# Spectral mixing and a squared-ReLU FFN on one Trainium2 core: the seven-product form for sixteen more token groups, complex sums and casts moved to DMAs

## The chip, the cores and the metric

The kernel runs on one core of one Trainium2 chip. The metric is the device time of one execution in microseconds (us); lower is better. The kernel before took 789.52 us (median of three runs, 789.43 to 789.87). The granted clock of TensorE was 1.000 in the profiled execution.

A core has five engines with a queue each, worked off in order: PE (TensorE, the matrix engine; PEld is its weight load), DVE (VectorE), ACT (ScalarE), POOL (GpSimd) and SP (SyncE, which issues most transfers here). They wait for one another through semaphores.

## The reference

```python
# x (8, 3008, 256), filt_r and filt_i (1505, 256), moe_w_in (256, 2048), moe_w_out (2048, 256), all float32
X = np.fft.rfft(x, axis=1)
Y = X * (filt_r + 1j * filt_i)[None, :, :]
y = np.fft.irfft(Y, n=3008, axis=1).astype(np.float32)
h = np.maximum(y.reshape(24064, 256) @ moe_w_in, 0.0)
out = (h * h @ moe_w_out).astype(np.float32)
```

Each of the eight batch elements is filtered along its 3008 positions; then all 24064 tokens go through a two-layer network whose activation is the squared ReLU.

## The kernel before, in words

**The FFN.** The tokens are worked off in 47 groups of 512. A group has eight *slots*, s = 8g + k. In slot k, `ffn_g1` (line 562) makes four matmuls of 512 columns, which give two of the sixteen 128-row tiles of the hidden layer; ACT applies the ReLU from PSUM into `h2` (line 566); `ffn_sq` squares the two tiles in place on DVE (line 570). The second layer runs one group late: in the slots of group g+1, `ffn_g2` (line 579) makes eight matmuls of 256 columns for group g in each slot, with a tile of `h2` as the weights and `sWout` as the moving operand; `ffn_out` copies the sum out of PSUM twice a group (line 590), and `store` issues its transfers (lines 610 and 612).

**The seven-product form.** For the groups in `SEVEN` (40 to 45 before), the second layer is written as a 2 x 2 by 2 x 2 block product: two halves of the tokens, two halves of the hidden rows, two halves of the output columns. `sums` makes four sums of blocks of `h2` on DVE (lines 643 to 652), and `make_t` makes the four sums of blocks of `sWout` once. `products` then forms seven products of sixteen matmuls of 128 columns each, instead of 64 of 256 columns (line 670). `PARTS` spreads them over eight slots, one slot later than `ffn_g2` would: slots 1 to 7 of group g+1 and slot 0 of group g+2. Two PSUM tiles, `psX` and `psY`, are held from the first product to the last. ACT copies four of the seven results out (lines 677 to 689), and DVE makes three additions (lines 686, 687, 692).

**The mixing.** It is a DFT in two factors (64 x 47), and every batch element passes five stages. x is loaded as float32 by SP (line 192) and cast to float16 by DVE (line 340). *Stage A* (`unit_a`, line 361) is the 47-point part; its output goes through DRAM (`write_u` line 344, `read_u` line 436) for a transposition. *Stage B* (`unit_b`, line 445) is the other factor for two of the 24 frequency classes at a time; DVE multiplies it by the filter (line 453), which gives `prod`, of which the partner's half stands in the other 64 partitions. Two DVE copies bring it across (lines 460 and 461), and `unit_s` adds (line 467): that is the sum of a complex product. *Stage P* (`unit_p`, line 496) goes back, ACT copies it out (line 498), and it passes through DRAM (`dZ`, line 501; `read_z`, line 514). *Stage Y* (`unit_y`, line 532) finishes and writes the tokens `yt` that `ffn_g1` reads.

**What sets the order.** The order is written out by hand: the last loop of the kernel goes through the slots, and in each it issues `ffn_g1`, the mixing work planned for place 0, the second layer of the group before, the mixing work of place 1, then `ffn_out`, `sums` and `ffn_sq`. `fft_plan(b)` gives each unit of batch element b a slot r counted from a start; the starts of b = 2 to 7 lie 48 slots, six groups, apart (b = 3 starts at slot 88). There stage A has the slots r = 6 to 13, `read_u` 14, stage B 19 to 37, `unit_p` two slots after its `unit_b`, `read_z` 40, stage Y 45 to 52. Batch element 0 is worked off before the loop, in a prologue; b = 1 is interleaved with the first groups. Stages A, B, P and Y share two PSUM banks (`psF`); `psH` has two buffers of two banks, `psO` two of one bank.

Of the kernel before, what the change touches and what calls it, by code (L numbers as in the profile page):

```python
# [110 lines left out]
def kernel(  # L111
# [32 lines left out]
    p_prod = ctx.enter_context(tc.tile_pool(name="p_prod", bufs=3))  # L144
    p_yf = ctx.enter_context(tc.tile_pool(name="p_yf", bufs=4))
# [3 lines left out]
    p_out = ctx.enter_context(tc.tile_pool(name="p_out", bufs=3))  # L149

# [33 lines left out]
    x32s = {}  # L184

    def load_x(b, c, pool=None, tag="x32", q=None):

        t = (pool or p_x32).tile([96, 8, D], F32, tag=tag, name=f"x32_{b}_{c}")
        q = q or nc.sync
        if b + 1 < B:  # L190
            v = xrows[b * S:b * S + 96 * NM, :].rearrange("(p m) d -> p m d", m=NM)
            q.dma_start(out=t, in_=v[:, 8 * c:8 * c + 8, :])
        else:
            v = xrows[b * S:b * S + S, :].rearrange("(p m) d -> p m d", m=NM)
            q.dma_start(out=t[0:80], in_=v[0:80, 8 * c:8 * c + 8, :])
            q.dma_start(out=t[80:94], in_=v[80:94, 8 * c:8 * c + 8, :])
        x32s[(b, c)] = t
# [3 lines left out]
    sC0 = const.tile([128, 1472], F16, name="sC0")  # L201
# [3 lines left out]
    sSA = sC0[0:94, 1280:1376]  # L205
    sSY = sC0[0:112, 1376:1470]
# [40 lines left out]
    nc.sync.dma_start(out=sC0[:, 704:1472], in_=dC0.ap()[:, 704:1472])  # L247
# [60 lines left out]
    def load_win():  # L308

        for k, c, n, pool, tag in ((0, 0, 768, p_ze, "ze"), (0, 768, 768, p_ze, "ze"),  # L310
                                   (0, 1536, 512, p_prod, "prod"), (1, 0, 768, p_ze, "ze"),
                                   (1, 768, 512, p_prod, "prod"), (1, 1280, 512, p_prod, "prod"),
                                   (1, 1792, 256, p_yf, "yf")):
            t = pool.tile([128, n], F32, tag=tag, name=f"win32_{k}_{c}")
            nc.sync.dma_start(out=t, in_=moe_w_in[128 * k:128 * k + 128, c:c + n])
            wins.append((t, k, slice(c, c + n)))
# [19 lines left out]
    x16s, us, uts, prods, zes, zts, yts = {}, {}, {}, {}, {}, {}, {}  # L336

    def cast_x(b, c, eng=nc.vector):
        t = p_x16.tile([94, 8, D], F16, tag="x16", name=f"x16_{b}_{c}")
        eng.tensor_copy(out=t, in_=x32s.pop((b, c))[0:94])  # L340
        x16s[(b, c)] = t

# [5 lines left out]
    def unit_a(b, a):  # L348

        c, i = divmod(a, 4)  # L350
        if i == 0:
            us[(b, c)] = p_u.tile([96, 8, D], F16, tag="u", name=f"u_{b}_{c}")
        ps = psF(f"psA_{b}_{a}")
        m = slice(2 * i, 2 * i + 2)
        if b == 1:
            nc.tensor.matmul(ps[0:96, :], s1[:, c // 2, :], xw16[(b, 2 * (c % 2))][:, m, :],
                             start=True, stop=False)
            nc.tensor.matmul(ps[0:96, :], s1[0:120, 2 + c, :], xw16[(b, 1)][0:120, m, :],
                             start=False, stop=True)
        else:  # L360
            nc.tensor.matmul(ps[0:96, :], sSA, x16s[(b, c)][:, m, :], start=True, stop=True)  # L361
        o = us[(b, c)][:, 2 * i:2 * i + 2, :]
        pv = ps[0:96, :].rearrange("p (a d) -> p a d", d=D)
        if a % 2 == 0:
            nc.scalar.copy(out=o, in_=pv)  # L365
        else:
            nc.vector.tensor_copy(out=o, in_=pv)  # L367
        if i == 3:
            write_u(b, c)
# [69 lines left out]
    def unit_b(b, p):  # L439
# [18 lines left out]
        if b > 0:  # L458
            yf = p_yf.tile([128, 2, D], F16, tag="yf", name=f"yf_{b}_{p}")
            nc.vector.tensor_copy(out=yf[0:64], in_=prod[64:128, 1])  # L460
            nc.vector.tensor_copy(out=yf[64:128], in_=prod[0:64, 1])
            prods[(b, p)] = prod, yf

    def unit_s(b, p):

        prod, yf = prods[(b, p)]
        nc.vector.tensor_add(out=yf, in0=prod[:, 0], in1=yf)  # L467
        prods[(b, p)] = yf
# [20 lines left out]
    def unit_p(b, p):  # L489
# [3 lines left out]
        yf = prods.pop((b, p))  # L493
# [12 lines left out]
    ztiles = [const.tile([112, 8, D], F16, name=f"zt_{c}") for c in range(4)]  # L506
# [3 lines left out]
    def read_z(b, c, ks=(0, 1)):  # L510
        zt = ztiles[c]
        v = dZ[b].rearrange("(q j) d -> q j d", j=NM)
        for k in ks:
            nc.sync.dma_start(out=zt[64 * k:64 * k + 48],
                              in_=v[48 * k:48 * k + 48, 8 * c:8 * c + 8, :])
        zts[(b, c)] = zt
# [51 lines left out]
    def ffn_sq(g, s):  # L568
        v = h2s[g][:, 2 * s:2 * s + 2, :]
        nc.vector.tensor_mul(out=v, in0=v, in1=v)  # L570
# [46 lines left out]
    def make_t():  # L617

        t = p_x32.tile([128, 4, 8, 128], F16, tag="x32", name="sT")
# [13 lines left out]
    def sums(g, k):  # L633
# [7 lines left out]
        t = p_x16.tile([128, 8, D], F16, tag="x16", name=f"sum_{g}_{k}")  # L641
# [17 lines left out]
    def products(g, k):  # L659

        f = sg[g]
        for p, m0, m1 in PARTS[k]:
# [12 lines left out]
            if p == 1:  # L675
                f["pu"] = p_prod.tile([128, 2, 2, 128], F32, tag="prod", name=f"pu_{g}")
                nc.scalar.copy(out=f["pu"][:, 0], in_=o)
            elif p == 6:
                f["u2"] = p_prod.tile([128, 2, 128], F32, tag="prod", name=f"u2_{g}")
                nc.scalar.copy(out=f["u2"], in_=o)  # L680
            elif p == 7:
                nc.scalar.copy(out=f["pu"][:, 1], in_=o)
            elif p == 2:
                f["top"] = p_out.tile([128, 2, 256], F32, tag="ost", name=f"top_{g}")
                f["bot"] = p_out.tile([128, 2, 256], F32, tag="ost", name=f"bot_{g}")
                nc.vector.tensor_add(out=f["top"][:, :, 0:128], in0=f["y"][:, 0], in1=f["pu"][:, 0])
                nc.vector.tensor_add(out=f["bot"][:, :, 128:256], in0=f["y"][:, 1], in1=f["pu"][:, 1])
            elif p == 4:
                nc.scalar.copy(out=f["bot"][:, :, 0:128], in_=o)
                store(g, 2, 2, f["bot"])  # L690
            elif p == 3:
                nc.vector.tensor_add(out=f["top"][:, :, 128:256], in0=o, in1=f["u2"])
                store(g, 0, 2, f["top"])

    def fft_plan(b):
# [11 lines left out]
        t0 = 2 if b == 1 else 6  # L707
        for a in range(12 if b == 1 else 0, 16):
            put(t0 + a // 2, a % 2, unit_a, b, a)
        put(10 if b == 1 else 14, 1, read_u, b)  # L710
        t0 = 14 if b == 1 else 19
        for p in range(12):
            r = t0 + (17 if b == 1 else 18) * p // 11
            put(r, 0, unit_b, b, p)
            put(r, 0, unit_s, b, p)
            put(r + 2, 1, unit_p, b, p)
        t0 = 34 if b == 1 else 40
        for c in range(4):
            put(t0, 1, read_z, b, c)
        if b + 1 < B:  # L720
            for c in range(2):
                put(t0 - 13, 1, load_x, b + 1, c)
            for c in range(4):
                r = t0 - 8 + 3 * c
                put(r, 1, cast_x, b + 1, c)
                if c < 2:
                    put(r, 1, load_x, b + 1, c + 2)
# [79 lines left out]
    SEVEN = range(40, NG - 1)  # L807
    work = {}
    for b in range(1, B):
        first = (b * S // TG) * SLOTS - (48 if b > 1 else 40)  # L810
        for (r, place), w in fft_plan(b).items():
            work[(first + r, place)] = w
# [49 lines left out]
```

## Time and profile before

| what | value |
|---|---|
| median of the runs (lowest, highest) | 789.52 us (789.43, 789.87) |
| the profiled execution's own time | 789.29 us |
| its span from first to last instruction | 787.2 us |
| around the span | 2.1 us |
| DMA traffic | 107.36 MB, mean 136 GB/s |
| SP's queue, share of 16 DMA engines | 46.9% |
| POOL busy, nearly all of it in the first 50 us | 23.6 us |
| loop over the slots, from its first matmul | 49.2 us on |

How to read it: the profile has the busy time of each engine, then groups of instructions by source line (busy time, mean duration of one in ns, the engine's idle time before them and what ended it), then the chain of work that ended last. A matmul's duration in it covers its whole way through the array, so that of a row of matmuls each starts long before the one ahead has ended. What a matmul costs TensorE is the distance from start to start, which the timeline shows. Beside POOL's own instructions, the issue of a DMA by POOL appears as an instruction, `DMA_DIRECT2D`.

### The profile page before, as it was taken

The numbers are of one execution on the slowest core, as the hardware profiler recorded it, in microseconds if no ns is written. First come the engines' busy times: TensorE is split into PE (matmuls) and PEld (weight loads), VectorE is DVE, ScalarE is ACT, GpSimd is POOL, SyncE is SP. The second block draws the span as 40 slices with busy tenths as digits, with TensorE's granted clock in tenths as the row PEclk, the third lists the DMA queues.
The fourth block names the chain that finished last, engine by engine and source line by source line (L and its number), as shares of the span: only waits on it lengthen the run. The fifth ranks groups of instructions, "written<-read, shape, count | busy, mean of one in ns | idle before, by whom it ended". The sixth has DMA issues, their size and how long they took to land.

```text
span 787.2 us, 15477 instructions
## 1 busy us (share of the span) xinstructions
PE 774.9 (98%) x6390; PEld 552.6 (70%) x6390; DVE 584.4 (74%) x943; ACT 558.5 (71%) x723; POOL 23.6 (3%) x36
## 2 busy tenths in 40 slices
PE   8989999999999999999999999999999999999998
PEld 5846667667676676867778677776767667677776
DVE  6866995579855897559965599556995569878884
ACT  3976776777777776767776777676777767777674
POOL 3800000000000000000000000000000000000000
PEclk9999999999999999999999999999999999999999
DMA  9995554345724467054571555525564342421011
GB/s 363 371 258 157 147 158 112 88 139 158 193 67 109 158 169 181 32 160 145 134 186 49 169 141 140 148 67 161 147 169 98 91 138 82 109 67 54 29 54 55
DMA packets 88574, 107.36 MB, mean 136 GB/s; under 512 B 6336, under 2 KB 79040, under 8 KB 84288
## 3 DMA queue, kind: packets, MB, share of 16 engines
q1 hardware_dynamic: 88296, 106.19, 46.9%
q8 instruction: 50, 0.82, 0.4%
q10 hardware_dynamic: 144, 0.18, 0.1%
q14 instruction: 20, 0.16, 0.1%
q0 software_dynamic: 64, 0.00, 0.0%
HBM read 58.12 MB, written 48.23 MB: 135 GB/s over the span
## 4 chain that ended last, share of the span: by engine, by line
PE 91%; DVE 6%; ACT 1%; DMA 1%; issue 0%; ACTq 0%; SPq 0%; DVEq 0%
PE psH L562 39%; PE psO L579 34%; PE psX L670 3%; PE psA L361 3%; PE psY L532 2%; PE psB L445 2%; PE psP L496 2%; PE psY L670 2%; DVE prod L453 2%; DVE h L570 2%; PE warm L268 1%; DMA wout<-in_moe_w_out_dram 1%; PE psf L287 1%; PE psf L290 1%; DVE yf L467 0%; ACT sF L298 0%
## 5 line engine op out<-in xcount | busy, mean ns | idle before, releaser
L566 ACT ACTIVATE h<-psH 128x1024 f16<-128x1024 f32 x376 | 384.9, 1025 | 183.1 <-PE psH L562 180.5
L562 PE MATMUL psH<-yt,sWin 128*128 128x512 f16 (+7 forms) x1728 | 386.9, 351 | 1.7 <-DVE yt L541 0.7
L579 PE MATMUL psO<-sWout,h 128*128 128x256 f16 x2624 | 339.2, 272 | 0.6 <-DVE h L570 0.6
L570 DVE TENSOR_TENSOR h<-h 128x1024 f16<-128x1024 f16 x376 | 251.9, 684 | 66.3 <-ACT h L566 65.6
L579 PEld LDWEIGHTS <-h 128*128 128x128 f16 x2624 | 253.3, 98 | 66.0 <-DVE h L570 0.9
L562 PEld LDWEIGHTS <-sWin 128*128 128x128 f16 x1728 | 157.7, 98 | 100.7 <-issue 3.4
L453 DVE TENSOR_TENSOR prod<-psB,sF 128x1024 f16<-128x1024 f32 x84 | 102.3, 1218 | 2.8 <-PE psB L445 2.7
L541 DVE CAST yt<-psY 128x376 f16<-128x376 f32 x62 | 34.0, 549 | 54.7 <-PE psY L532 54.6
L367 DVE CAST u<-psA 96x512 f16<-96x512 f32 x50 | 34.3, 687 | 47.3 <-PE psA L361 45.1
L498 ACT CAST ze<-psP 128x512 f16<-128x512 f32 x84 | 49.1, 585 | 17.2 <-PE psP L496 14.7
L590 ACT COPY ost<-psO 128x512 f32<-128x512 f32 (+1 forms) x84 | 48.8, 581 | 7.7 <-PE psO L579 4.3
L532 PE MATMUL psY<-sC,zt 112*128 112x94 f16 x512 | 42.3, 205 | 1.0 <-DMA zt<-dZ 1.0
L532 PEld LDWEIGHTS <-zt 112*128 112x128 f16 x512 | 34.9, 98 | 11.1 <-issue 1.2
L467 DVE TENSOR_TENSOR yf<-prod,yf 128x512 f16<-128x512 f16 x84 | 35.7, 425 | 2.9
L361 PE MATMUL psA<-x,sC 94*96 94x512 f16 x96 | 36.6, 382 | 0.0
L445 PE MATMUL psB<-ut,sSB 128*128 128x256 f16 x192 | 36.5, 273 | 0.0
L496 PE MATMUL psP<-yf,sSP 128*128 128x256 f16 x168 | 32.1, 272 | 0.5 <-DVE prod L453 0.3
L445 PEld LDWEIGHTS <-sSB 128*128 128x128 f16 x192 | 18.5, 98 | 19.5
L539 ACT CAST yt<-psY 128x376 f16<-128x376 f32 x66 | 30.9, 468 | 1.6 <-issue 1.3
L340 DVE CAST x<-x 94x2048 f16<-94x2048 f32 x24 | 29.2, 1216 | 0.0
L365 ACT CAST u<-psA 96x512 f16<-96x512 f32 x50 | 28.6, 572 | 0.0
L670 PEld LDWEIGHTS <-sum 128*128 128x128 f16 x384 | 23.8, 98 | 4.9
(88 smaller groups left out, 395.3 us busy)
## 6 DMA issues: line engine op xcount, KB each, us to landing
x<-in_x_dram SPq DMA_DIRECT2D x20, 768.0 KB
zt<-dZ SPq DMA_DIRECT2D x64, 192.0 KB
dU<-u SPq DMA_DIRECT2D x28, 384.0 KB
dZ<-ze SPq DMA_DIRECT2D x28, 384.0 KB
out_dram<-ost SPq DMA_DIRECT2D x58, 128.0 KB
ut<-dU SPq DMA_DIRECT2D x7, 1024.0 KB
out_dram<-ost SPq DMA_DIRECT2D x27, 256.0 KB
xw<-in_x_dram SPq DMA_DIRECT2D x6, 1024.0 KB
```

What stands on the lines that cost most here:

```text
L361: nc.tensor.matmul(ps[0:96, :], sSA, x16s[(b, c)][:, m, :], start=True, stop=True)
L445: nc.tensor.matmul(ps[:, i * D:(i + 1) * D], sSB[:, 2 * p + i, :], uts[b][:, 2 * p + i, :], start=True, stop=True)
L453: nc.vector.tensor_mul(out=prod, in0=ps.rearrange("p (a d) -> p a d", d=D).unsqueeze(1).to_broadcast([128, 2, 2, D]), in1=sF[:, :, 2 * p:2 ...
L496: nc.tensor.matmul(ps[:, i * D:(i + 1) * D], sSP[:, 2 * p + i, :], yf[:, i, :], start=True, stop=True)
L498: nc.scalar.copy(out=zes[(b, c)][:, 2 * i6:2 * i6 + 2, :], in_=ps.rearrange("p (a d) -> p a d", d=D))
L532: nc.tensor.matmul(ps[:, 94 * jj:94 * jj + 94], zt[:, 4 * (g % 2) + jj, dt * 128:(dt + 1) * 128], sSY, start=True, stop=True)
L562: nc.tensor.matmul(ps[:, i, o:o + n], sWin[:, dt, jt * 128:(jt + 1) * 128], yts[b][:, dt, r:r + n], start=(dt == 0), stop=(dt == 1))
L566: nc.scalar.activation(out=h2[:, 2 * s:2 * s + 2, :], in_=ps, func=AF.Relu)
L570: nc.vector.tensor_mul(out=v, in0=v, in1=v)
L579: nc.tensor.matmul(pso[g][:, t % 2, :], h2s[g][:, jt, t * 128:(t + 1) * 128], sWout[:, jt, :], start=(jt == 0), stop=(jt == NJT - 1))
L590: nc.scalar.copy(out=ost[:, h0:h0 + step, :], in_=pso[g][:, h0:h0 + step, :])
L670: nc.tensor.matmul(o[:, t, :], f[p][:, q, 128 * t:128 * t + 128], sg["w"][p][:, q, :], start=(m == 0 and p in (1, 2)), stop=(q == 7), skip ...
```

## The change

- **Seven products for more groups.** `SEVEN` gains the odd groups 9 to 39, sixteen in all. A plain group follows each of them, so that slot 0 of the group after a seven-product group has `ffn_g1` alone, and slot 0 of the next has the last part of `products` and the first of `ffn_g2`.
- **Squares over two slots.** `ffn_sq` does four tiles in every second slot, but for the last group.
- **Adding DMAs.** The two copies and the addition on DVE after the filter product go. POOL issues two DMAs of 64 x 512 elements each that add one half of `prod` onto the other in place. `unit_p` comes four slots after its `unit_b` instead of two, and `prod` has four buffers instead of three.
- **x cast by its DMAs.** SP's loads of x and DVE's casts go. POOL issues eight DMAs for each batch element (for the last one sixteen) that read float32 and write float16, one after each of eight of the `unit_b` of the batch element before.
- **Moves.** Stages A and B and `read_u` come one slot earlier, `read_z` one slot later (41), and the read of its last quarter at slot 47, because three tiles `zt` serve instead of four. For b = 1, stage B is spread over 15 slots instead of 17.
- **Memory.** The first and the seventh result, and the sixth, are copied by ACT straight into the tiles `top` and `bot` that are stored, and DVE adds there. The sums lie in the pool that held the loads of x. One constant is loaded in two parts.

The core of the diff:

```diff
@@ def load_x
-    def load_x(b, c, pool=None, tag="x32", q=None):
-        t = (pool or p_x32).tile([96, 8, D], F32, tag=tag, name=f"x32_{b}_{c}")
-        q = q or nc.sync
+    def load_x(b, k):
+        c, i = divmod(k, 2)
+        if i == 0:
+            x16s[(b, c)] = p_x16.tile([96, 8, D], F16, tag="x16", name=f"x16_{b}_{c}")
+        t = x16s[(b, c)][:, 4 * i:4 * i + 4, :]
+        m = slice(8 * c + 4 * i, 8 * c + 4 * i + 4)
         if b + 1 < B:
             v = xrows[b * S:b * S + 96 * NM, :].rearrange("(p m) d -> p m d", m=NM)
-            q.dma_start(out=t, in_=v[:, 8 * c:8 * c + 8, :])
+            nc.gpsimd.dma_start(out=t, in_=v[:, m, :])
...
-    def cast_x(b, c, eng=nc.vector):
-        t = p_x16.tile([94, 8, D], F16, tag="x16", name=f"x16_{b}_{c}")
-        eng.tensor_copy(out=t, in_=x32s.pop((b, c))[0:94])
-        x16s[(b, c)] = t
@@ def unit_b
         if b > 0:
-            yf = p_yf.tile([128, 2, D], F16, tag="yf", name=f"yf_{b}_{p}")
-            nc.vector.tensor_copy(out=yf[0:64], in_=prod[64:128, 1])
-            nc.vector.tensor_copy(out=yf[64:128], in_=prod[0:64, 1])
-            prods[(b, p)] = prod, yf
-
-    def unit_s(b, p):
-        prod, yf = prods[(b, p)]
-        nc.vector.tensor_add(out=yf, in0=prod[:, 0], in1=yf)
-        prods[(b, p)] = yf
+            for i in range(2):
+                nc.gpsimd.dma_start(out=prod[64 * i:64 * i + 64, 0],
+                                    in_=prod[64 - 64 * i:128 - 64 * i, 1],
+                                    accum_op=mybir.AluOpType.add)
@@ def ffn_sq
-        v = h2s[g][:, 2 * s:2 * s + 2, :]
+        n = 1 if g == NG - 1 else 2
+        if (s + 1) % n:
+            return
+        v = h2s[g][:, 2 * (s + 1 - n):2 * s + 2, :]
         nc.vector.tensor_mul(out=v, in0=v, in1=v)
@@ def products
             if p == 1:
-                f["pu"] = p_prod.tile([128, 2, 2, 128], F32, tag="prod", name=f"pu_{g}")
-                nc.scalar.copy(out=f["pu"][:, 0], in_=o)
+                f["top"] = p_out.tile([128, 2, 256], F32, tag="ost", name=f"top_{g}")
+                nc.scalar.copy(out=f["top"][:, :, 0:128], in_=o)
...
             elif p == 2:
-                f["top"] = p_out.tile([128, 2, 256], F32, tag="ost", name=f"top_{g}")
-                f["bot"] = p_out.tile([128, 2, 256], F32, tag="ost", name=f"bot_{g}")
-                nc.vector.tensor_add(out=f["top"][:, :, 0:128], in0=f["y"][:, 0], in1=f["pu"][:, 0])
-                nc.vector.tensor_add(out=f["bot"][:, :, 128:256], in0=f["y"][:, 1], in1=f["pu"][:, 1])
+                for v, i in ((f["top"][:, :, 0:128], 0), (f["bot"][:, :, 128:256], 1)):
+                    nc.vector.tensor_add(out=v, in0=f["y"][:, i], in1=v)
@@ def fft_plan
-        t0 = 2 if b == 1 else 6
+        t0 = 2 if b == 1 else 5
...
-        put(10 if b == 1 else 14, 1, read_u, b)
-        t0 = 14 if b == 1 else 19
+        put(10 if b == 1 else 13, 1, read_u, b)
+        t0 = 14 if b == 1 else 18
         for p in range(12):
-            r = t0 + (17 if b == 1 else 18) * p // 11
+            r = t0 + (15 if b == 1 else 18) * p // 11
             put(r, 0, unit_b, b, p)
-            put(r, 0, unit_s, b, p)
-            put(r + 2, 1, unit_p, b, p)
-        t0 = 34 if b == 1 else 40
+            if b + 1 < B and 2 <= p < 10:
+                put(r, 0, load_x, b + 1, p - 2)
+            put(r + 4, 1, unit_p, b, p)
+        t0 = 34 if b == 1 else 41
         for c in range(4):
-            put(t0, 1, read_z, b, c)
...
+            put(t0 if c < 3 else t0 + 6, 1, read_z, b, c)
@@ the loop
-    SEVEN = range(40, NG - 1)
+    SEVEN = [g for g in range(9, NG - 1) if g % 2 or g >= 40]
```

## Prediction

> **What bounds the kernel now.** I read the busy times first, then the groups, then TensorE's timeline in a stretch without mixing work.
>
> ```profile
> PE 774.9 (98%) x6390; PEld 552.6 (70%) x6390; DVE 584.4 (74%) x943; ACT 558.5 (71%) x723; POOL 23.6 (3%) x36
> L579 PE MATMUL psO<-sWout,h 128*128 128x256 f16 x2624 | 339.2, 272 | 0.6 <-DVE h L570 0.6
> L570 DVE TENSOR_TENSOR h<-h 128x1024 f16<-128x1024 f16 x376 | 251.9, 684 | 66.3 <-ACT h L566 65.6
> L453 DVE TENSOR_TENSOR prod<-psB,sF 128x1024 f16<-128x1024 f32 x84 | 102.3, 1218 | 2.8 <-PE psB L445 2.7
> L467 DVE TENSOR_TENSOR yf<-prod,yf 128x512 f16<-128x512 f16 x84 | 35.7, 425 | 2.9
> L340 DVE CAST x<-x 94x2048 f16<-94x2048 f32 x24 | 29.2, 1216 | 0.0
> ```
>
> TensorE is never idle for long, so time comes off only where its own work does. In the timeline (start, length, instructions) the next two fences show a plain slot and slots of groups 42 to 45, which are in the seven-product form already:
>
> ```profile
> 206.00 1.03 PE L562 MATMUL psH<-yt,sWin 128*128 128x512 f16 x4
> 206.86 1.04 PE L579 MATMUL psO<-sWout,h 128*128 128x256 f16 x8
> 207.73 1.03 PE L562 MATMUL psH<-yt,sWin 128*128 128x512 f16 x4
> ```
>
> ```profile
> 742.79 1.03 PE L562 MATMUL psH<-yt,sWin 128*128 128x512 f16 x4
> 743.66 0.61 PE L670 MATMUL psX<-sT,sum 128*128 128x128 f16 x8
> 744.10 0.50 PE L670 MATMUL psY<-sT,sum 128*128 128x128 f16 x6
> 744.44 0.38 PE L562 MATMUL psH<-yt,sWin 128*128 128x512 f16 x1
> ```
>
> A plain slot is 1.74 us from start to start, one with 14 small products 1.65. The third view is busy time by stretch, for one group under seven products without mixing and for two groups in stage B (columns: stretch, its length, then PE, PEld, DVE, ACT):
>
> ```profile
> 736.21:749.37 13.16, 13.16 (x147) 9.39 (x145) 10.81 (x15) 9.33 (x13) 0.00 (x0) 1.00 0.13 42
> 269.22:285.08 15.86, 15.86 (x117) 11.16 (x114) 15.45 (x29) 11.87 (x16) 0.00 (x0) 1.00 0.67 183
> 285.08:300.94 15.86, 15.86 (x117) 11.12 (x115) 15.35 (x26) 11.62 (x15) 0.00 (x0) 1.00 0.52 135
> ```
>
> DVE is 97% busy in stage B. Four sums more would not fit there; that is why the change must first empty DVE.
>
> **What the Trainium skill says.** "TensorE: Matmul & The Clock Gate", section "Wait — 56ns, not 53.3ns?": a warm matmul starts N/2.4 ns + 2.5 ns after the one ahead. The trace agrees: 216, 109 and 56 ns from start to start at 512, 256 and 128 columns, weight loads hidden. "DMA: Bandwidth & Descriptors", section "Anatomy of one DMA": a DMA from GpSimd takes 2.0 us plus its bytes over 436 GB/s; 2.15 us for 64 KB. Its section "Latency and other measured facts" puts about 1 us on the issue. The trace has only two tiny ones, at its busy start: 617 and 484 ns to issue, 6.2 us to land. "SBUF — State Buffer", section "Who interferes with whom": a two-input DVE operation does not keep GpSimd from writing descriptors, a copy or cast within SBUF can. The change removes those copies; no row of before shows the two together.
>
> **The change, part by part.**
>
> *Seven products.* A plain group takes 8 x 1.738 = 13.90 us, a seven-product group 13.16 (window above): 0.74 less; by the gaps, 64 x 0.109 - 112 x 0.056 = 0.70. Sixteen groups: **-11.9**. The short slot (`ffn_g1` alone, 0.87) and the long one (0.87 + 12 x 0.056 + 0.87 = 2.4) move work, and add none. ACT needs 1.02 for a ReLU in the short slot, but the two `psH` buffers carry 0.15 over: nothing.
>
> *DVE.* Off: casts 29.2, copies 24.3 + 24.1, additions 35.7, together 113 us; squares in pairs cost a step of 1.135 (as the sums have) against 2 x 0.602: -3. On: 64 sums x 1.218 = 78, 48 additions x 0.42 = 20. DVE falls from 584 to about 555, but it waits beside TensorE, so this is worth only what DVE holds up now. That is in b = 1, where the timeline has
>
> ```profile
> 93.36 0.38 PE L496 MATMUL psP<-yf,sSP 128*128 128x256 f16 x2 [0.27 <-DVE prod L453]
> 113.67 0.39 PE L579 MATMUL psO<-sWout,h 128*128 128x256 f16 x2 [0.60 <-DVE h L570]
> ```
>
> From start to start these cost 0.44 and 0.76; with DVE's backlog gone: **-1.2**.
>
> *DVE where seven products meet stage B.* For b = 3 to 7 one group (13, 19, ... 37) has its products in r = 25 to 32, with five `unit_b`. I add up both queues from r = 24 on (DVE steps 1.135 for squares, sums, products with the filter; PE 0.87 `ffn_g1`, 0.22 each B and P, parts at 0.056 a matmul). Slots start at 0, 1.1, 3.1, 5.1, 7.0, 8.9, 11.0, 12.7, 14.7. DVE: square 0.4, prod 1.5, sum 2.65, sum 3.9, square 5.0, prod 6.2, sum 7.3, prod 8.5 to 9.7, square, sum, prod 11.9, square, two additions 14.2, prod 14.9 to 16.1. It runs up to 2 us late, yet each sum is ready (the first at 3.9 for 4.8, the second at 5.1 for 6.5). What is late is the PSUM bank: the `unit_b` of r = 29 needs the prod done at 9.7 and comes at 9.8; that of r = 32 comes at 15.6 and needs 16.1. **+0.5** x 5 = 2.5 (0 to 1.2 each). The other ten groups meet stage A or Y, where DVE has 0.6 or 0.47 us a slot instead: nothing, covered by 0.3 us at least.
>
> *Adding DMAs.* Off TensorE's path while they land before `unit_p`: four slots, about 7.2 us after the prod; 5.1 and 4.8 in r = 30 and 31 above, where prod is late. Price: from 2 x 0.5 + 2.15 = 3.2 to 2 x 1.0 + 6.2 = 8.2. An early landing gains nothing, since `unit_p` has its place in PE's queue. I take 2 x 0.9 and 2.6 for the landing, as SP's write of `dZ` has it: 4.4, with 0.3 lost in some of the tight places: **+1.5** (0 to 4). What queues behind: the next adding DMA waits for its prod, and the loads of x stand between; unit_p's wait holds PE's whole queue. DVE waits before it reuses a `prod` buffer for the DMAs of four units earlier, whose `unit_p` is through by then: nothing.
>
> *x cast by DMAs.* 24 loads leave SP's queue, whose waits cost nothing now. On POOL each comes behind two adding DMAs, so three issues in each 3.3 us (1.64 slots of 2.0). At 0.9 us they fit. Needed 20 slots later: nothing.
>
> *Stage P to Y.* Here a cover shrinks. Before (b = 3), the last `unit_p` ends at 301.1; `dZ` is written, and the first two reads of `zt` follow:
>
> ```profile
> 301.75 0.38 SPq L501 DMA_DIRECT2D dZ<-ze  x1
> 302.24 1.71 SPq L612 DMA_DIRECT2D out_dram<-ost  x3
> 304.05 3.81 SPq L514 DMA_DIRECT2D zt<-dZ  x8
> 310.48 0.33 PE L532 MATMUL psY<-sC,zt 112*128 112x94 f16 x4
> ```
>
> By the trace's semaphore updates `dZ` landed at 304.75 and the second read at 308.23, 2.25 us early (1.1 to 2.3 over b = 2 to 7). After, `unit_p` stands in r = 40, a short slot, and r = 41 to 44 are slots with products (1.76, 1.65, 1.65, 1.65): from its end to `unit_y` it is 7.4 us instead of 9.4. ACT has the ReLU of that slot ahead of its copy: 1.3 until `dZ` is issued, then 0.4 + 2.6 + 0.35 + 2.95 (medians) = 7.6. **+0.3** with the scatter, for six batch elements: 1.8 (0 to 1.2 each). The read at slot 47 has four slots of some 2 us for 3.3: nothing.
>
> *Rest.* One more small load in the prologue, results copied straight into `top`: same counts, nothing.
>
> Sum: 789.3 - 11.9 - 1.2 + 2.5 + 1.5 + 1.8 = 782.0 in the profiled execution's own time; the median of the runs stands 0.2 higher, **782.2**.
>
> **The rivals.**
>
> *No stall* (0.16): queues fit as written, 789.5 - 13.1 = 776.4. For it: groups 41 to 45 run without a wait. Against: in none of them is there mixing.
>
> *The waits take it* (0.16): both ends above, 6 + 4 + 7.2 = 17.2 instead of 5.8, some of which fall together; with 11.5, 787.9. For it: a DVE 2 us late and a cover of 7.4 us for 7.6.
>
> *Slower: POOL's issue is the bound* (0.16). From b = 1 to 6 there are eight spells of three issues in 3.29 us. Above 1.10 us an issue, POOL falls behind by 8 x (3x - 3.29), of which `unit_p` has 7.2 - 4.6 = 2.6 to give; the rest TensorE waits. It decides from 1.26 us: 8 x 0.49 - 2.6 = 1.3 us, six times, which is the 7.3 gained. At 1.4 us: 8 x 0.91 - 2.6 = 4.7, six times 28, 810. For it: 1 us by the skill, for one DMA of unknown shape. Against: 0.5 to 0.6 in the trace.
>
> **How the numbers follow.** My forecast has 0.52. About 0.2% (1.6 us) is what a measurement of this kernel can tell from no change. The second rival lies half within that (0.07), nearly all else of it below (0.08). Faster 0.52 + 0.16 + 0.08 = 0.76, same 0.07, slower 0.17. The range goes from the stall-free end, 776, to the upper end of the waits, 790; outside are the slower rival and little else.
>
> **What would show it.** Slots of 1.65 us with parts of products in groups 10 to 40, and 1.74 elsewhere: the saving. Idle time of PE at `unit_b` put down to the filter product: the bank. At `unit_y`, to `zt`: the shrunk cover. At `unit_p`, to a DMA into `prod`, with POOL's `DMA_DIRECT2D` over 1.1 us: the slower rival. I am wrong if a DVE operation or a matmul changes its own duration beside POOL's DMAs, or if landings of the adding DMAs take over 5 us.

## The result, and the profile after

| | before | after |
|---|---|---|
| median of the runs (lowest to highest) | 789.56 us (789.43 to 789.87) | 789.68 us (787.49 to 791.16) |
| ratio, 95% interval | | 0.9999 (0.9975 to 1.0023) |
| the profiled execution's own time; its span | 789.29; 787.2 us | 791.16; 789.1 us |

No change that can be measured, where 782.2 was forecast. The page of the changed kernel first, the busy times and the groups that answer to those shown of before:

```profile
PE 766.1 (97%) x7158; PEld 552.1 (70%) x7158; DVE 548.0 (69%) x594; ACT 559.4 (71%) x755; POOL 193.2 (24%) x260
L564 DVE TENSOR_TENSOR h<-h 128x2048 f16<-128x2048 f16 (+1 forms) x192 | 229.8, 1197 | 110.5 <-ACT h L557 107.3
L457 POOL DMA_DIRECT2D prod<-prod x168 | 141.2, 998 | 470.3 <-DVE prod L450 464.1
L573 PE MATMUL psO<-sWout,h 128*128 128x256 f16 x1600 | 206.3, 272 | 0.0
L450 DVE TENSOR_TENSOR prod<-psB,sF 128x1024 f16<-128x1024 f32 x84 | 102.4, 1220 | 20.6 <-PE psB L442 18.8
L195 POOL DMA_DIRECT2D x<-in_x_dram x40 | 46.0, 1151 | 0.0
```

What the change was to remove is gone: 1024 matmuls of 256 columns (1792 of 128 columns stand in their place), and the casts, copies and additions on DVE. No operation shown has become longer (products with the filter 1220 ns, before 1218). TensorE is busy 8.8 us less, and the span is not shorter: it waits more. The waits of TensorE (total us, times, longest us; waits of the start-up and of b = 1 left out):

```profile
PE psY L523 <- DMA zt<-dZ: 8.7, 8, 1.7
...
PE psA L358 <- ACT u L362: 1.6, 6, 0.3
PE psY L666 <- DVE bot L681: 1.5, 5, 0.3
```

And TensorE's timeline at one place of each kind (start, length, instructions, in brackets the idle time before):

```profile
212.34 1.03 PE L553 MATMUL psH<-yt,sWin 128*128 128x512 f16 x4
...
213.98 1.03 PE L553 MATMUL psH<-yt,sWin 128*128 128x512 f16 x4
216.20 0.33 PE L523 MATMUL psY<-sC,zt 112*128 112x94 f16 x4 [1.20 <-DMA zt<-dZ]
...
241.58 0.38 PE L358 MATMUL psA<-x,sC 94*96 94x512 f16 x1 [0.28 <-ACT u L362]
...
284.67 0.38 PE L666 MATMUL psY<-sWout,sum 128*128 128x128 f16 x4 [0.31 <-DVE bot L681]
```

A slot of seven products takes 1.64 us from start to start (212.34 to 213.98), as forecast. The wait at 216.20 costs more than the bracket says, since a matmul's length covers its way through the array: four matmuls of 512 columns take 4 x 0.216, so those at 213.98 should have let the next start at 214.84, and TensorE lost 1.36. In this way, start to start less what the columns take, I added up both executions (the table has the difference from before; of the +0.9, 0.6 stand at three `unit_p` and 0.4 at one later `unit_y`):

| where | forecast | measured |
|---|---|---|
| sixteen groups in seven products | -11.9 | -11.9 |
| b = 1 and the groups up to 8 | -1.2 | 0.0 |
| the first stage Y unit, r = 45, b = 2 to 7 | +1.8 | +7.8 (1.36, 1.27, 1.84, 1.55, 0.54, 1.20) |
| stage A, r = 9, b = 3 to 7 | 0 | +2.2 (5 x 0.44) |
| seven products beside stage B, b = 3 to 7 | +2.5 | +2.4 (5 x 0.47) |
| adding DMAs at `unit_p`, and the rest | +1.5 | +0.9 |
| first slot reached later (prologue) | 0 | +0.6 |
| sum | -7.3 | +2.0 |

The spans differ by 1.9. The prologue's 0.6 is scatter: the first slot starts at 49.2 before and 49.8 after, and between 48.9 and 49.8 in the traces of all experiments but e5. The profiled execution is the slowest of the four of the changed kernel (787.49 to 791.16), so its waits are rather long ones; in e2 and e3 below, where the transfers between stages P and Y are as in the changed kernel, the waits at r = 45 add up to 5.7 and 6.6 instead of 7.8. Of 30 runs of the kernel before, taken beside the experiments, 18 lie at 789.1 to 790.0 with a granted clock of 0.999 or 1.000, and 12 at 790.8 to 791.5 with 0.998.

### The profile page after: what moved, and what is told of

It is laid out like the page before. It is cut to its first block, busy times and chain, and to the rows that moved or that the text cites. A ratio compares the mean times of both kernels' runs of the same rounds, so it can differ in the third digit from the quotient of the medians.

```text
span 789.1 us, 17241 instructions
## 1 busy us (share of the span) xinstructions
PE 766.1 (97%) x7158; PEld 552.1 (70%) x7158; DVE 548.0 (69%) x594; ACT 559.4 (71%) x755; POOL 193.2 (24%) x260
## 4 chain that ended last, share of the span: by engine, by line
PE 76%; DMA 10%; DVE 7%; ACT 3%; issue 2%; POOL 1%; SPq 0%; DVEq 0%; ACTq 0%
PE psH L553 32%; PE psO L573 21%; PE psX L666 6%; PE psY L666 5%; DMA zt<-dZ 4%; DMA dZ<-ze 3%; DVE prod L450 3%; PE psY L523 3%; PE psA L358 2%; DVE h L564 2%; DMA f<-in_filt_i_dram 2%; PE psB L442 2%; ACT h L557 2%; PE psP L487 2%; PE psf L291 1%
## 5 line engine op out<-in xcount | busy, mean ns | idle before, releaser
L564 DVE TENSOR_TENSOR h<-h 128x2048 f16<-128x2048 f16 (+1 forms) x192 | 229.8, 1197 | 110.5 <-ACT h L557 107.3
L457 POOL DMA_DIRECT2D prod<-prod x168 | 141.2, 998 | 470.3 <-DVE prod L450 464.1
L553 PEld LDWEIGHTS <-sWin 128*128 128x128 f16 x1728 | 155.7, 98 | 100.2 <-issue 3.4
L573 PE MATMUL psO<-sWout,h 128*128 128x256 f16 x1600 | 206.3, 272 | 0.0
L573 PEld LDWEIGHTS <-h 128*128 128x128 f16 x1600 | 154.0, 98 | 35.1 <-issue 0.2
L450 DVE TENSOR_TENSOR prod<-psB,sF 128x1024 f16<-128x1024 f32 x84 | 102.4, 1220 | 20.6 <-PE psB L442 18.8
L666 PEld LDWEIGHTS <-sum 128*128 128x128 f16 x1408 | 87.2, 98 | 15.9 <-issue 2.2
L666 PEld LDWEIGHTS <-h 128*128 128x128 f16 x1056 | 65.6, 98 | 17.2 <-issue 2.7
L666 PE MATMUL psX<-sT,sum 128*128 128x128 f16 x704 | 50.1, 219 | 0.0
L195 POOL DMA_DIRECT2D x<-in_x_dram x40 | 46.0, 1151 | 0.0
L584 ACT COPY ost<-psO 128x512 f32<-128x512 f32 (+1 forms) x52 | 29.8, 574 | 7.1 <-PE psO L573 6.2
L666 PE MATMUL psY<-sT,sum 128*128 128x128 f16 x352 | 34.0, 219 | 0.0
```

The source lines that it names most:

```text
L195: nc.gpsimd.dma_start(out=t, in_=v[:, m, :])
L450: nc.vector.tensor_mul(out=prod, in0=ps.rearrange("p (a d) -> p a d", d=D).unsqueeze(1).to_broadcast([128, 2, 2, D]), in1=sF[:, :, 2 * p:2 ...
L457: nc.gpsimd.dma_start(out=prod[64 * i:64 * i + 64, 0], in_=prod[64 - 64 * i:128 - 64 * i, 1], accum_op=mybir.AluOpType.add)
L553: nc.tensor.matmul(ps[:, i, o:o + n], sWin[:, dt, jt * 128:(jt + 1) * 128], yts[b][:, dt, r:r + n], start=(dt == 0), stop=(dt == 1))
L573: nc.tensor.matmul(pso[g][:, t % 2, :], h2s[g][:, jt, t * 128:(t + 1) * 128], sWout[:, jt, :], start=(jt == 0), stop=(jt == NJT - 1))
L666: nc.tensor.matmul(o[:, t, :], f[p][:, q, 128 * t:128 * t + 128], sg["w"][p][:, q, :], start=(m == 0 and p in (1, 2)), stop=(q == 7), skip ...
```

## The experiments

My theory from the two traces: the scheme brings its 11.9 us, and three waits made by the order of the slots take it back. First come one mend for each wait, and all three together. Times of the kernel before beside these runs: 789.94 (30 runs), then 789.33 (27), 789.70 (11), 789.79 (9).

**e1, the cover of stage P to Y restored.** The last `unit_p` goes from the short slot 40 back to 39, and `read_z` to 40 (its last quarter stays at 47; the line for that is left out here):

```diff
-            put(r + 4, 1, unit_p, b, p)
-        t0 = 34 if b == 1 else 41
+            put(r + (3 if b > 1 and p == 11 else 4), 1, unit_p, b, p)
+        t0 = 34 if b == 1 else 40
...
```

> The last unit_p of a batch element (b = 2 to 7) goes back to slot 39 and read_z to slot 40, nothing else changes. Theory of the three waits: the six waits of unit_y for zt (7.8 us in the profile of the changed kernel) are gone or under 0.3 us each, the stage A and psY waits stay (2.2 and 2.4 us), so about 781.5 us. Rival, contention: POOL's adding and casting DMAs make the transfers of dZ slow wherever they stand, then dZ takes 3.5 us or more to land and at least 4 us of the waits stay, 786 or above. Rival, no saving: products amid mixing save less than 0.74 us a group, then the time stays at 789 whatever happens to the waits.

Measured: 784.46 us (782.25 to 785.73), ratio 0.9925 (0.9907 to 0.9942). That is 5.2 below the changed kernel by the medians, not the 8 that were expected; the profiled executions (the slowest there, the fastest here) differ by 8.9. The timeline of SP's queue for b = 3 in the changed kernel, and then in this one, with the unit of TensorE that needs the data:

```profile
302.28 1.27 SPq L606 DMA_DIRECT2D out_dram<-ost  x3
304.01 0.38 SPq L492 DMA_DIRECT2D dZ<-ze  x1
304.49 5.86 SPq L505 DMA_DIRECT2D zt<-dZ  x6
```

```profile
300.69 0.37 SPq L492 DMA_DIRECT2D dZ<-ze  x1
301.18 1.69 SPq L606 DMA_DIRECT2D out_dram<-ost  x3
302.97 3.81 SPq L505 DMA_DIRECT2D zt<-dZ  x6
...
308.30 0.33 PE L523 MATMUL psY<-sC,zt 112*128 112x94 f16 x4
```

In the changed kernel the slot's output stores stand ahead of the write of `dZ`; it lands 3.77 us after its issue ends. Here it stands first, as it did before the change, and lands after 3.05. The transfers as a whole are no quicker for that: from the issue of `dZ` to the landing of the second read they take 7.06 us here and 7.05 in the changed kernel (means of b = 2 to 7). What has changed is the time for them. `unit_y` starts 8.26 us after stage P ends instead of 7.4, and `dZ` is issued 0.65 us after stage P instead of 1.34. The second read lands at 307.71, 0.58 ahead of `unit_y` (0.17 to 1.06 over b = 2 to 7). No wait at r = 45 is left; those of stage A and of the products are unchanged (2.2 and 2.0).

**e2, the third product in one piece.**

```diff
-((4, 8, 16), (3, 0, 4)), ((3, 4, 16),))
+((4, 8, 16),), ((3, 0, 16),))
```

> The four matmuls of the third product that stood in slot 7 of a seven-product group go to its last part. Theory of the three waits: they waited for DVE's second addition, which reads the same psY half; the five waits of 0.47 us in the groups that meet stage B go, 787.3 us against 789.7, and the zt waits stay. Rival, DVE is simply behind: the wait turns up one instruction later, at the unit_b of the next slot or in the last part itself, and the time stays within 0.5 us of the changed kernel.

Measured: 790.22 us (788.29 to 791.84), ratio 1.000 (0.999 to 1.001). The wait for `bot` is gone, and in its place the waits have

```profile
PE psB L442 <- DVE prod L450: 1.8, 5, 0.4
```

Start to start that is 0.52, five times, at the `unit_b` of r = 32. So DVE is behind there, and what meets it first waits: the rival came true. Moving the matmuls moves the wait and doesn't shorten it.

**e3, stage A's first unit after the short slot.** Both units of slot 9 stand behind the FFN's second layer:

```diff
-            put(t0 + a // 2, a % 2, unit_a, b, a)
+            r = t0 + a // 2
+            put(r, 1 if b > 1 and r == 9 else a % 2, unit_a, b, a)
```

> In the slot after the short one, both unit_a go behind the products instead of one ahead of them. Theory of the three waits: the five waits of 0.44 us for ACT's copy in stage A go, since the bank is asked for 0.9 us later; 787.5 us. Rival, ACT is short of time there: the second unit_a or the next ReLU waits as long, no change.

Measured: 787.97 us (785.11 to 790.76), ratio 0.9969 (0.9958 to 0.998). The five waits at `psA` are gone, and the products and stage A have no new ones. (At `unit_p` this trace has waits of 0.40, 1.17 and 0.99 us for adding DMAs, where the changed kernel's has 0.6 in all; they come later in the batch element, and whether the edit brought them isn't shown.) On ACT in the changed kernel:

```profile
240.03 1.02 ACT L557 ACTIVATE h<-psH 128x1024 f16<-128x1024 f32 x1 [0.20 <-PE psH L553]
240.95 0.57 ACT L362 CAST u<-psA 96x512 f16<-96x512 f32 x1
```

The copy that frees the PSUM bank stands behind the ReLU of the short slot, ends at 241.52, and the `unit_a` that needs the bank starts at 241.58. Between it and the unit before, the short slot has only the four matmuls of `ffn_g1` for TensorE.

**e4, all three.**

> The three edits together. Theory of the three waits: they add up, 7.8 + 2.4 + 2.2 = 12.4 us, about 777.5 us, which is what sixteen groups at 0.74 us promise. Rival, contention: 784 or above. Rival, no saving from products amid mixing: 788 or above.

Measured: 783.45 us (782.5 to 783.89), ratio 0.9913 (0.99 to 0.9927). That is 1.0 below e1, where e3 alone promised 1.7. Whether it is less than the sum isn't shown: the granted clock was 1.000 in all four runs of e1, but 0.998 in three of the four of e4, and in the profiled one TensorE ran at half speed from 48.9 to 52.3, which cost about 1.0 us there. The expected 777.5 is missed in any case. Some 5 us of waits are left from group 9 on: 2.35 at `unit_b` for DVE, 1.4 at `unit_p`, 1.07 at `zt`.

The next four ask what the parts of the change do by themselves, where the late landing of `dZ` comes from, and whether the theory can be used.

**e5, the complex sums back on DVE** (e1, with two copies and an addition for the two adding DMAs, `unit_p` at r + 3; `prod` has three buffers instead of four, and two for `yf` come in):

```diff
-            for i in range(2):
-                nc.gpsimd.dma_start(out=prod[64 * i:64 * i + 64, 0],
-                                    in_=prod[64 - 64 * i:128 - 64 * i, 1],
-                                    accum_op=mybir.AluOpType.add)
+            yf = p_yf.tile([128, 2, D], F16, tag="yf", name=f"yf_{b}_{p}")
+            nc.vector.tensor_copy(out=yf[0:64], in_=prod[64:128, 1])
+            nc.vector.tensor_copy(out=yf[64:128], in_=prod[0:64, 1])
+            nc.vector.tensor_add(out=prod[:, 0], in0=prod[:, 0], in1=yf)
```

> The kernel with the cover restored (784.5), but the complex sums back on VectorE (two copies and an addition instead of two adding DMAs). Theory: in the five seven-product groups that meet stage B VectorE has 3 products of 1.14 us and about 3.1 us of sums, squares and additions in the work of about 5.2 us of TensorE time, and is already late by 0.5 us at one point a group; 0.29 + 0.29 + 0.40 = about 0.96 us more a stage-B unit, 5 to 6 units a group, cannot be hidden, so each of the five groups is 4 to 5 us longer, plus the plain stage-B groups, where VectorE was 97% busy already: 800 to 808 us. Rival: the sums did not need to leave VectorE, the queues absorb them: 784 to 786 us. A result above 798 says that the adding DMAs are what makes the seven-product form possible beside stage B.

Measured: 830.03 us (827.51 to 837.28), ratio 1.0522 (1.0486 to 1.0559). Its waits:

```profile
PE psY L667 <- DVE bot L682: 15.6, 5, 3.1
PE psB L443 <- DMA ut<-dU: 8.8, 6, 2.2
PE psP L488 <- DVE prod L451: 8.3, 8, 1.4
```

The first and third rows are the expected cost: each of the five groups is 4.7 to 5.1 us longer than in e1, where the scheme saves 0.74. So beside stage B the scheme pays only with DVE freed of the sums. But 800 to 808 us were expected. Of the 45 us between the two traces these groups are 24.5; 9.8 (start to start) are the second row, 4.1 lie before the first slot (it starts at 53.8; the reading of `zt` ends later there, and I didn't follow it further), and 4.9 come from TensorE running at half speed (last section). The second row I had not expected. The loads of x on POOL's queue used to stand between adding DMAs; with those gone nothing holds them, and POOL issues them as soon as stage A lets go of their buffers:

```profile
246.44 1.01 POOL L196 DMA_DIRECT2D x<-in_x_dram  x2 [82.07 <-PE psA L359]
```

There they run beside the transfers of `dU` and `ut`, and TensorE waits for `ut`; no run moved these loads alone.

**e6, the DMAs without the new groups.**

```diff
-    SEVEN = [g for g in range(9, NG - 1) if g % 2 or g >= 40]
+    SEVEN = range(40, NG - 1)
```

> The changed kernel without the sixteen new seven-product groups (only groups 40 to 45 stay in that form, as before): what is left of the change is the adding DMAs, the casting loads, the squares over two slots, the moved buffers, and the stage order one slot earlier. Theory: these are worth next to nothing for the time; the two waits of the second batch element (0.76 and the like) go or stay within 1 us, and the stage P to Y cover is shortened by the earlier slots only a little since the slots are all 1.74 us: 788.5 to 790 us. Rival (contention: the adding and casting DMAs slow VectorE or the matmuls, or their landings hold TensorE): over 792 us. If it is at 789 to 790, the 13 us of new waits in the changed kernel come from the short and long slots of the new groups and not from the DMAs.

Measured: 789.32 us (789.01 to 790.74), ratio 0.9994 (0.9987 to 1.0002). Of the waits at `zt` one of 0.2 us is left in r = 45, and none in stage A at r = 9. So the large new waits come with the new groups; the rest of the change by itself, adding and casting DMAs included, costs and brings nothing that can be measured, though DVE falls to 461.6 us.

**e7, a store behind `dZ`.** In slot 39 the copy out of PSUM and its pair of output stores wait for the next slot (the line that makes the list `late` is left out):

```diff
+        if k == 0 and late:
+            ffn_out(*late.pop())
         if g > 0 and g - 1 not in SEVEN:
-            ffn_out(g - 1, k)
+            if s > 78 and (s - 40) % 48 == 39 and g < 41:
+                late.append((g - 1, k))
+            else:
+                ffn_out(g - 1, k)
```

> The changed kernel with the second pair of output stores of the plain group in slot 39 of each batch element moved behind the write of dZ on SyncE's queue. Theory A (the stores ahead of dZ in the queue are what makes it land 3.8 to 4.1 us after its issue instead of 2.6): dZ lands 1 to 1.5 us earlier, the waits at zt in the slot of the first stage Y unit fall from 1.2 to 1.8 us each to about 0.3, and the time from 789.7 to about 783 to 785.5. Theory B (only the short slots have taken the cover away; the stores share the DMA engines wherever they stand): the stores now delay the reads of zt instead, the waits stay above 1 us, 788 to 790 us.

Measured: 790.84 us (787.85 to 795.7), ratio 1.0016 (1.0003 to 1.003). Theory A is wrong: it had the waits at about 0.3 each and the time at 785.5 or below. SP's queue for b = 3:

```profile
303.64 0.37 SPq L492 DMA_DIRECT2D dZ<-ze  x1
304.13 2.22 SPq L606 DMA_DIRECT2D out_dram<-ost  x3
306.45 2.71 SPq L505 DMA_DIRECT2D zt<-dZ  x6
```

`dZ` does land sooner (2.8 us after its issue ends), but the first read is issued at 306.45 instead of 304.49, so the two reads run side by side, and the second lands 3.2 after its own issue instead of 2.7. From the issue of `dZ` to the second landing it is 7.0 us (mean of six), in the changed kernel 7.05. Six waits of 0.74 to 1.42, 6.5 in all, are left; that is no less than in e3 (6.6). So the order in SP's queue is not what costs the time, and of these edits only e1's, more time between stages P and Y, took the waits away.

**e8, five more groups** (e1 and e3, and groups 10, 16, ... 34):

```diff
-    SEVEN = [g for g in range(9, NG - 1) if g % 2 or g >= 40]
+    SEVEN = [g for g in range(9, NG - 1) if g % 2 or g % 6 == 4 or g >= 40]
```

> The changed kernel with the cover restored, the first stage A unit of the slot behind the short slot moved to the slot's other half, and five more groups (10, 16, 22, 28 and 34) in the seven-product form. Theory: each mend keeps its gain (5.3 and 1.7 us) and each added group takes its 0.74 us off, 3.7 in all, since these groups meet stages A and P where VectorE has room: 789.7 - 5.3 - 1.7 - 3.7 = 779 us. Rival (VectorE and the DMAs fill up where two such groups follow one another, and new waits take it): 782.5 to 785 us, no better than the two mends.

Measured: 779.3 us (776.68 to 783.12), ratio 0.9875 (0.9854 to 0.9896), as expected, and below every run of both kernels. Of the waits at `zt` and `psA`, 10 us in the changed kernel, there is left

```profile
PE psY L523 <- DMA zt<-dZ: 1.6, 3, 1.0
```

and, idle times again, 1.4 for DVE's addition and 0.2 in stage A. (The added groups meet the slots r = 1 to 8, which is the end of stage Y and stage A, not stage P as the expectation has it.)

**e9 and e10, how far it goes.** `if g % 6 or g >= 40` adds groups 14, 20, ... 38; then `SEVEN = range(9, NG - 1)`, every group.

> The kernel of 779.3 us (cover restored, stage A unit moved, groups 10, 16, ... 34 added) with groups 14, 20, 26, 32 and 38 in the seven-product form too; of groups 10 to 39 only 12, 18, 24, 30 and 36 stay plain. Their products fall into the last units of stage B and stage P, where VectorE is busy for 7.3 of 14.6 us in that kernel's trace; four sums and three additions put 6.1 us on it: 13.4 of 13.8. Theory (a group is worth its 0.74 us wherever VectorE's sum of work fits into the group's own time): 779.3 - 5 x 0.74 = 775.6 us. Rival (VectorE comes out of the group before 100% busy and late, so work added behind it cannot be caught up and delays the last stage P units and dZ): no gain, 779 to 784 us.

> Every group from 9 to 45 in the seven-product form. Added to the kernel just described: groups 12, 18, 24, 30 and 36, whose products meet the first half of stage B. VectorE is busy there for 9.1 of 14.6 us in the trace of the 779.3 us kernel; 6.1 us more make 15.2 in a group of 13.8, and the group behind it is full already (16.65 us of 16.68). Theory (VectorE's sum of work is the bound where it does not fit): each such group takes 0.74 off and brings 1.4 us or more of waits, 5 x 0.7 = 3 us worse than the kernel without them: about 778 to 782 us if that is at 775.6. Rival (the queues absorb it): about 772 us.

Measured: e9 784.25 us (783.2 to 787.55), ratio 0.9936 (0.9919 to 0.9952); e10 782.35 us (782.06 to 782.84), ratio 0.9905 (0.9891 to 0.9919). My theory fails for e9: the sum of DVE's work fits (13.3 us busy in 15.4), and yet 5 us are lost against e8. Its waits name the DMAs:

```profile
PE psP L487 <- DMA prod<-prod: 5.6, 7, 1.3
PE psY L523 <- DMA zt<-dZ: 5.1, 5, 1.5
```

In b = 4 the last product with the filter ends at 387.88, POOL issues its adding DMAs only at 389.64 (0.3 us behind the product in 82 of the 84 units; why it is late here isn't clear), and `unit_p` waits until 393.67. In the group ahead, with stage B, the DMA engines are 94% busy; adding DMAs there take up to 6.4 us to land, loads of x up to 7.6. But in e8 they take nearly as long, and there `unit_p` hardly waits for them (0.1 us): counted from the product, they land after 3.4 to 7.0 us in e8 and 3.4 to 7.4 in e9. What has shrunk is the cover again. In e8 the last `unit_p` of a batch element is due 5.1 us behind its product and the one before 7.0, in e9 3.4 to 5.2 and 5.0 to 6.0 (b = 3 to 7). The slots are shorter, and these products end 2.1 to 3.3 us behind their `unit_b`, in e8 1.7: DVE is late there, as the rival has it (779 to 784 us). e10 is 1.9 us faster than e9, where 3 us slower was expected: DVE's addition is late by 1.19 to 1.40 us in each of five groups, as the sum of its work says, but it was late by 0.47 already, so a group brings 0.9 of new waits for the 0.74 it saves, and the other waits (6.3 us for adding DMAs, 2.1 at `zt`) are fewer than in e9.

**e11 and e12, the loads of x moved out of stage B** in e9 and e10:

```diff
-                put(r, 0, load_x, b + 1, p - 2)
+                put(44 + p if b > 1 else r, 0, load_x, b + 1, p - 2)
```

> The kernel of 784.25 us (groups 12, 18, ... 36 plain, all others seven-product), with the casting loads of x for the next batch element moved out of stage B (where the trace has the DMA engines 94% busy) into slots 46 to 53, where they are 30 to 56% busy; each is still 7 slots ahead of its use. In that kernel TensorE waited 7.4 us at stage P for adding DMAs and 4.7 us at stage Y for zt. Theory (the adding DMAs land late because the loads of x fill the DMA engines and stand in POOL's queue between them): the 7.4 us at stage P go, 784.3 - 7.4 = 777 us, and about 775.6 if dZ, which follows the last stage P unit, is on time as well. Rival (VectorE is late there, so the adding DMAs are issued late whatever the loads do): the waits at stage P stay, 782 to 785 us.

> The same move of the loads in the kernel with every group from 9 to 45 in the seven-product form (782.35 us; there 6.3 us of waits at stage P for adding DMAs, 6.8 us for VectorE at the additions of the products). Theory: the waits at stage P go, those for VectorE stay: 782.35 - 6.3 = 776 us. Rival (VectorE is late and issues the adding DMAs late): 781 to 783 us.

Measured: 816.32 us (815.95 to 817.71), ratio 1.0335 (1.0321 to 1.0349), and 817.24 us (814.68 to 820.18), ratio 1.0344 (1.0319 to 1.0368). Both expectations missed, for a reason that the timeline of POOL's queue and the waits of e11 show:

```profile
302.11 4.67 POOL L195 DMA_DIRECT2D x<-in_x_dram  x8
```

```profile
PE psY L523 <- DMA zt<-dZ: 29.5, 7, 6.9
```

I had moved the loads in the program, not in time: behind the last adding DMA nothing holds POOL, and all eight go out at once in the slots r = 38 to 40, eight to thirteen slots ahead of where I put them, and just ahead of `dZ`, which then lands 8.9 to 11.2 us after its issue. At stage P itself the wait falls by half and the adding DMAs land in 2.9 us (median) instead of 3.7. (About 11 us of the loss are TensorE at half speed behind the long waits; see the last section.) So the loads have a part in how late the adding DMAs land. At the last `unit_p` waits of 1.47 and 1.17 us stay all the same, where the DMAs land 4.8 and 4.5 us behind the product and 3.4 are there. What the move would bring without the collision isn't shown; holding the loads in slots 46 to 53 by a wait of their own was not tried.

## Why the prediction was wrong

*Seven products, -11.9:* right. Slots with products alone take 1.65 us in the groups amid the mixing as well, and e8's five further groups brought what was computed for them.

*Stage P to Y, +1.8:* **the step that failed**; it measured 7.8. The cover that I worked out, 7.4 us, was right (7.38 in b = 3: 311.32 - 302.67 - 1.27). The chain of transfers that has to fit into it was not: "1.3 until `dZ` is issued, then 0.4 + 2.6 + 0.35 + 2.95 (medians) = 7.6" came to 7.8 to 9.1, 8.55 in the mean, and TensorE starts 0.14 behind the landing. A sum of medians leaves out every delay that comes now and then. The kernel before could have told: there the same stretch, from the issue of `dZ` to the second landing, took 6.5 to 7.6 us over b = 2 to 7, where the medians add up to 6.3.

In the changed kernel it took 6.3 and 6.5 in b = 2 and 6, as summed up. In b = 2 the stores held SP's queue, and `dZ` was issued 2.3 us after stage P instead of 1.3; in b = 7 the second read took 3.8 us to land instead of 2.95. In b = 3 to 5 the write of `dZ` landed after 3.77, 3.94 and 4.11 instead of 2.6, some 4 us of the 6 that the forecast was short. The cause isn't the order in SP's queue: in e6 the stores stand ahead of `dZ` in the same way, and it lands in 2.6 to 2.8 in all six. The trace of the changed kernel shows another one. The DMA traffic from 304.1 to 308.2 (b = 3), in 40 slices, and then from 590.1 to 593.1 (b = 6):

```profile
GB/s 519 310 310 120 10 0 0 0 180 280 270 270 275 280 270 270 285 285 275 275 295 140 20 20 25 20 20 145 100 300 105 460 305 260 170 80 40 80 40 0
q8 instruction: 1, 0.02, 2.5%
```

```profile
GB/s 0 0 0 0 0 0 0 0 0 0 82 253 300 273 294 307 273 287 314 273 287 300 273 287 246 232 225 171 191 164 369 431 232 328 382 328 492 55 110 0
```

In b = 3 the write runs at some 280 GB/s, then at 20, a fourteenth: 720 of its 768 packets are through at 306.5, and the last 48, a sixteenth, come one after another until 307.7. One of the 16 DMA engines is late with its share. What kept it is a fetch of the kernel's own instructions on queue 8, one packet of 16 KB that takes 1.66 us from 304.17; in b = 6 none falls into the write. In the changed kernel, e2 and e3, `dZ` took 3.65 to 4.11 in b = 3 to 5, with a fetch of 0.9 to 1.8 us beside the write each time, and 2.5 to 2.7 in b = 2, 6 and 7, where none delayed it. No experiment moved a fetch, so this is read from the packets and not shown by a change. e1 shows that the term as a whole was the cover: with 0.9 us more of it, and an issue 0.7 us earlier, all six waits are gone, whatever delays the transfers. My bound from above, 7.2, was nearer than the value that I took.

*Stage A, "nothing, covered by 0.3 us at least":* wrong by 2.2. I checked DVE there and, for ACT, only the two buffers of `psH`. What came late was another instruction in ACT's queue, the copy of `unit_a` behind the short slot's ReLU, and with it a bank of `psF`. e3 shows it.

*b = 1, -1.2:* not there. The wait of 0.76 for DVE is gone, but stage P of b = 1 now waits twice 0.44 for its bank, and stage Y of b = 1 meets stage A of b = 2, which comes one slot earlier (0.37 and 0.32). The same waits stand in e6, where no new group is.

*DVE beside stage B, +2.5:* right in size (2.4), and right that DVE is behind by that much; the place was another. The wait appears at the products, which wait for DVE's addition; only in e2 does it stand at the `unit_b` of r = 32, which the forecast named. (In the sum for DVE's busy time the squares should have -13 instead of -3, 184 pairs at 0.07; the 555 given there is right with it, and 548 came.)

*Adding DMAs, +1.5:* the right order; 0.6 at three `unit_p`. They land 3.4 us (median) from the start of their issue; with 1.0 of issue that leaves 2.4, and the Trainium skill, "DMA: Bandwidth & Descriptors", section "Anatomy of one DMA", gives 2.15 as an estimate for 64 KB from its formula. But 24 of the 168 took over 5 us, up to 7.2, which I had named as a sign of being wrong; the four slots up to `unit_p` covered nearly all of them. The slower rival was far off: POOL's issue is 998 ns long, but issues overlap. Three in a row step by 2.26 us, against 3.29 available:

```profile
266.69 1.65 POOL L457 DMA_DIRECT2D prod<-prod  x2 [2.05 <-DVE prod L450]
267.73 1.15 POOL L195 DMA_DIRECT2D x<-in_x_dram  x1
268.95 1.65 POOL L457 DMA_DIRECT2D prod<-prod  x2
```

So the second rival came true, "the waits take it" (787.9), through one of the three waits that it named and another, in stage A, that I had priced at nothing.

## What to carry to other kernels

A scheme that shortens slots also shortens every cover that is counted in slots: list the round trips through DRAM that span them, and price each from its longest times in the trace, measured from end to end, not from a sum of medians of its parts. When an engine's work is moved out of the way, look at each queue that frees a shared buffer in the shortest slot, not only at the engine that the change is about. And where waits eat a gain, mend the waits one at a time: here a few moved lines and five more groups turned no change into 779.3 us.

## What the runs showed of the hardware

- An issue of an adding DMA (64 KB within SBUF) is 998 ns long on POOL in the trace, of a casting load (192 KB) 1151 ns. But the next issue starts 0.52 us behind an adding DMA, and mostly 1.22 us behind a load that another adding DMA follows (medians of the changed kernel). Loads that follow one another start 0.50 us apart in e5 and 0.51 in e11 (medians), though each is 0.51 us long in e5 and 1.15 in e11. So the length of an issue is no measure of what it costs the queue. A place in POOL's queue is a place in an order, not in time.
- A fetch of instructions can hold up a transfer. With one of 16 KB (1.4 to 1.7 us) beside it, the write of `dZ` (384 KB) landed 1.1 to 1.5 us later in b = 3 to 5 of the changed kernel than in b = 2, 6 and 7 without one; in b = 3, it landed at 308.16, behind the 48 late packets of one DMA engine.
- TensorE ran at half speed after long waits. In e5 this came in three of the five waits of 3.1 us (idle in the trace; 3.3 from start to start less the columns), from 401.1, 602.5 and 701.5 on, for 3.41 us each: four matmuls of 512 columns came 0.43 us apart instead of 0.216, and each time cost 1.6 us. In e11 it came in all five waits of 5.2 to 7 us, was there when work began again, and lasted 3.4 to 5.6 us of work, which cost 1.8 to 2.7 us each. The Trainium skill, "TensorE: Matmul & The Clock Gate", section "Part 1: The HAM clock gate", puts the fall at about 3.4 us of idle, and under "Wait — 56ns, not 53.3ns?" the step at half clock at 426.7 ns; the step agrees, the idle time is a little under. So a long wait cost up to 2.7 us more than its length.
